# The opening of a delta-rule attention + maxout-FFN kernel: inverse norms, the first transposed solution and the first weights in another order

## The chip, the cores and the metric

The kernel runs on one core of one Trainium2 chip. The metric is device time in microseconds (us), from launch to the last store. The engines are TensorE (PE, matrix products), VectorE (DVE), ScalarE (ACT), GpSimd (POOL) and SyncE (SP, which here only issues transfers). Each works through its own queue of instructions in order; they meet at semaphores. ACT and POOL can issue transfers too.

## What is computed

Two layers follow one another. The first is a delta rule: for each of 4 x 8 heads a 48 x 48 state is carried over 768 tokens. The second is a feed-forward layer (FFN) with the maximum of three products.

```python
k_n = k / (norm(k) + 1e-06)
for t in range(S):
    y[t] = q[t] @ state
    v_old = k_n[t] @ state
    state = state + beta[t] * outer(k_n[t], v[t] - v_old)
x = y.transpose(0, 2, 1, 3).reshape(B * S, H * D)          # 3072 x 384
h = maximum(maximum(x @ w1, x @ w2), x @ w3)               # 384 -> 768
out = h @ w_out                                            # 768 -> 384
```

## The kernel before, in words

**Chunks and groups.** Tokens are taken in chunks of 64. A unit is one chunk of half of the batch; two units make a chunk c of all heads, two chunks make a group m of 512 tokens of the FFN (there are 6 groups). Inside a chunk the recurrence is a triangular system: with A the products of the keys among themselves, u = (I + A)^-1 (scaled values - keys x state). `gram` makes A and the masked products of queries and keys (`pts`) on PE, `turn` transposes keys and queries on PE for that, and ACT or DVE copy each result out of PSUM.

**The solve.** The inverse is found on DVE for blocks of 32 x 32, all heads and blocks at once: each of the 128 partitions holds one block of 1024 numbers. `solve(m)` first takes the key norms from the blocks' diagonals (`norm`), makes the inverse squares times beta (`bl`), scales the blocks with them (L547), puts `bl` on the diagonal of the result (L538), and then runs column by column: a product into `tmp` (L561), a subtraction from the result `y_bl` (L565). For group 0 the blocks are solved only in halves of 16 (`FINE`), so there are 15 steps instead of 31, and the off-diagonal parts are made on PE from the halves: `halves_z` (p_e, L685), `halves_u` (p_f, written back negated at L700). The 32-wide parts of a chunk come from `join_z` (p_z, L713) and `join_u` (p_j, L726, L728). These read the solution in `ut[c]`, and a transposed copy of parts of it: `fine[c]`, made by `halves_t(c)`, and `t1[c]`, made by `turn_t1(c)`, both with the 32 x 32 transposing of DVE.

**From the blocks to ut.** For group 0 the whole 128 x 1024 solution is transposed on DVE (L573), and `placed(cc, i)` copies a quarter of chunk cc into `ut[cc]` (L505, 32 partitions x 512 elements). Chunk 0 is copied at the end of `solve(0)`, by DVE and ACT; chunk 1 in pieces further on. For later groups this goes through DRAM.

**Values.** The system works with unnormalised keys, so the values are scaled by the key norms: `first_norms` transposes the norms of group 0 (L311, DVE), `scale(c)` multiplies v_t by them on POOL (L296). `new(c)` then makes u (p_u, L771) from v_t and ut, `to_y` the chunk's y (p_y, L813), `to_x` transposes y on PE (p_x, L832), ACT copies it to `xt`, and the FFN's products (p_h, L1224) read that. `step` adds to the state (p_s, L794; st, L801).

**Weights.** The weights come as pieces of 128 x 384 in a 64-bit format (`fetch`, on the queues of SP or POOL). The generator `weights()` converts one piece a turn: three ACT operations (L247 to L249) into `mant` and `up`, two buffers each; then `joined` shifts on DVE (L259) and adds on POOL (L263). `joined` of a piece is called in the turn of the next one.

**Order.** All of it is under a schedule written by hand: the program order is the order of each engine's queue. After the first loads, lines 1309 to 1375 write out the opening; then `ffn(0)` is a generator, and after each of its steps i the tables (`FIRST`, `EARLY_LINKS`, `CONVERTED`) say what else is put in: S a step of `solving`, M a masking (DVE), T and P a `turn` and a `gram` of queries, e, f, d, z, j, u, y, x, s, k, q the links of the recurrence. `solve(1)` runs on DVE meanwhile; its y_p lies in PSUM.

PSUM tiles of the opening come from `ps_two`, three buffers of two banks; each p_t, p_g, p_e and so on takes one and holds it until it has been copied out. The square tiles (`square`, 17 buffers) hold the products A (`ats`), the masked ones (`pts`), the `fine` tiles and the FFN's h.

## Time and profile before

Three runs: 506.24 us median (505.86 to 509.44). The profile is one execution.

| | us |
|---|---|
| time of the profiled execution | 506.9 |
| span of its instructions | 505.2 |
| PE busy | 484.0 (96%) |
| DVE busy | 361.1 (71%) |
| POOL busy | 187.1 (37%) |
| ACT busy | 169.4 (34%) |

How to read the lines: an engine's line in the 40 slices has one digit for each slice of 12.6 us, the busy share in tenths; PEclk is the clock that was granted to PE, in tenths of full speed. In the timeline each row is: start, duration, engine, line of the kernel, operation, out<-in by the program's names, shape, how many; in brackets the idle time of the engine before it and what ended it. In the chain of waits each piece has start, duration and the engine, tile and line that held the end up. What an engine names as its releaser is inferred from the last semaphore; where that one had long been done, it was another.

### The profile page before, as it was taken

How to read it: one execution, taken by the hardware profiler on the slowest of the kernel's cores; microseconds unless marked ns; L12 is line 12 of the kernel's file. 1: busy time of each engine (PE TensorE's matmuls, PEld its weight loads, DVE VectorE, ACT ScalarE, POOL GpSimd, SP SyncE). 2: the span in 40 equal slices, each digit the busy share in tenths (PEclk: the TensorE clock that was granted, in tenths of full speed). 3: DMA queues.
4: the chain of work that ended last, by engine and by line, in shares of the span. 5: the costliest groups of instructions: out<-in, count | busy, mean ns of one | idle time of the engine just before them, and what ended most of it. 6: DMA issues, size and time to landing. Idle time of an engine off the chain costs nothing.

```text
span 505.2 us, 18676 instructions
## 1 busy us (share of the span) xinstructions
PE 484.0 (96%) x8064; PEld 338.0 (67%) x8064; DVE 361.1 (71%) x835; ACT 169.4 (34%) x320; POOL 187.1 (37%) x311
## 2 busy tenths in 40 slices
PE   7678989999999999999999999999999999999996
PEld 6467767855566555565565565555797457998895
DVE  5888799787996441799652999565998874468753
ACT  5585664885422142210152200242201032212210
POOL 7434472793391935770395880501000020000000
PEclk9855899999999999999999999999999999999999
DMA  8937869864045934544584652744224230340002
GB/s 114 205 50 214 195 142 160 198 181 137 3 120 134 191 72 77 146 119 117 112 156 104 158 137 74 149 72 96 64 54 90 47 86 15 85 94 1 0 18 47
DMA packets 109121, 53.50 MB, mean 106 GB/s; under 512 B 92208, under 2 KB 102864, under 8 KB 109040
## 3 DMA queue, kind: packets, MB, share of 16 engines
q1 hardware_dynamic: 97280, 31.78, 31.0%
q0 software_dynamic: 9216, 19.85, 16.5%
q8 instruction: 63, 1.03, 0.9%
q10 hardware_dynamic: 2544, 0.69, 0.8%
q14 instruction: 18, 0.15, 0.1%
HBM read 39.17 MB, written 13.11 MB: 103 GB/s over the span
## 4 chain that ended last, share of the span: by engine, by line
PE 76%; DVE 11%; ACT 4%; DMA 3%; SPq 3%; issue 2%; POOL 0%; DVEq 0%; ACTq 0%; POOLq 0%
PE p_h L1224 28%; PE p_o L985 13%; PE p_o L1262 12%; PE p_c L1163 5%; DVE tmp L561 3%; PE p_g L415 2%; PE p_m L905 2%; PE p_u L771 2%; PE p_k L743 2%; DVE y_p L565 2%; DMA kmore<-in_k_dram 2%; PE p_y L813 2%; PE p_s L794 2%; PE p_q L743 1%; PE p_j L726 1%
## 5 line engine op out<-in xcount | busy, mean ns | idle before, releaser
L1224 PE MATMUL p_h<-xt,w_sb 128*128 128x512 f32 (+1 forms) x450 | 186.8, 558 | 0.6 <-ACT xt L839 0.6
L1224 PEld LDWEIGHTS p_h<-xt,w_sb 128*128 128x128 f32 x450 | 82.4, 193 | 69.2 <-issue 61.6
L1238 DVE TENSOR_TENSOR h<-h,p_h 128x512 f32<-128x512 f32 (+1 forms) x42 | 25.5, 607 | 46.8 <-PE p_h L1224 46.3
L565 DVE TENSOR_TENSOR y_bl<-y_bl,tmp 128x31 f32<-128x31 f32 (+20 forms) x139 | 50.4, 363 | 4.8
L561 DVE TENSOR_TENSOR tmp<-x_bl,y_bl 128x31 f32<-128x31 f32 (+20 forms) x139 | 48.8, 351 | 3.9
L1262 PE MATMUL p_o<-wo_sb,h 128*128 128x384 f32 x144 | 48.9, 490 | 0.0
L373 POOL DMA_DIRECT2D turned<-in_q_dram x72 | 39.3, 554 | 4.6 <-POOL turned L368 3.1
L1262 PEld LDWEIGHTS p_o<-wo_sb,h 128*128 128x128 f32 x144 | 26.7, 190 | 17.2
L1234 ACT ACTIVATE h<-p_h 128x512 f32<-128x512 f32 x24 | 14.3, 597 | 69.2 <-PE p_h L1224 69.2
L263 POOL TENSOR_TENSOR w_sb<-mant,up 128x384 int32<-128x384 int32 x18 | 19.0, 1054 | 39.5 <-DVE mant L259 37.8
L415 PEld LDWEIGHTS p_g<-kqt 48*64 48x64 f32 x1216 | 24.5, 142 | 9.2 <-issue 6.3
L415 PE MATMUL p_g<-kqt 48*64 48x64 f32 (+1 forms) x1216 | 27.7, 241 | 0.9 <-ACT kqt L344 0.8
L1268 ACT COPY o_sb<-p_o 128x384 f32<-128x384 f32 x12 | 5.8, 479 | 62.6 <-PE p_o L1262 56.5
L801 DVE TENSOR_TENSOR st<-st,p_s 48x768 f32<-48x768 f32 (+1 forms) x18 | 17.1, 949 | 12.7 <-PE p_s L794 12.4
L399 DVE TENSOR_TENSOR pt<-p_g,mask 128x512 f32<-128x512 f32 x20 | 13.8, 690 | 17.0 <-PE p_g L415 16.9
L598 POOL DMA_DIRECT2D ut<-y_d x4 | 2.6, 653 | 60.6 <-DMA y_d<-y_bl 60.6
L148 POOL DMA_DIRECT2D v_t<-in_v_dram x14 | 11.6, 832 | 35.3 <-PE p_u L771 35.3
L368 POOL MEMSET turned<- 128x96 f32 x18 | 3.3, 191 | 49.4 <-DVE kqt L389 49.4
L771 PEld LDWEIGHTS p_u<-v_t,ut 64*64 64x64 f32 x768 | 13.5, 141 | 8.4 <-issue 7.3
L432 ACT COPY at<-p_g 128x512 f32<-128x512 f32 x22 | 12.8, 585 | 17.4 <-DVE pt L399 15.4
L373 POOL DMA_DIRECT2D turned<-in_k_dram x32 | 17.5, 556 | 1.2 <-POOL turned L368 1.2
L1163 PE MATMUL p_c<-xt,w_sb 128*128 128x256 f32 x72 | 17.7, 379 | 0.0
(239 smaller groups left out, 907.3 us busy)
## 6 DMA issues: line engine op xcount, KB each, us to landing
w_bits<-in_moe_w_dram SPq DMA_DIRECT2D x9, 384.0 KB, 6.2
w_bits<-in_moe_w_dram POOLq DMA_DIRECT2D x9, 384.0 KB, 5.7
turned<-in_q_dram POOLq DMA_DIRECT2D x72, 48.0 KB, 2.8
out_dram<-o_sb SPq DMA_DIRECT2D x36, 96.0 KB, 2.3
y_x<-y SPq DMA_DIRECT2D x32, 96.0 KB, 3.0
qall<-y_x SPq DMA_DIRECT2D x32, 96.0 KB, 2.8
v_t<-in_v_dram POOLq DMA_DIRECT2D x14, 192.0 KB, 5.0
at_d<-at SPq DMA_DIRECT2D x72, 32.0 KB, 3.0
```

What stands on the lines that cost most here:

```text
L263: nc.gpsimd.tensor_tensor(out=dst.bitcast(I32), in0=mant_v.bitcast(I32), in1=up_v, op=ALU.add)
L373: (queue, nc.gpsimd)[i].dma_start(out=t[p0 : p0 + 32, bb, at : at + NP * 2 * D].rearrange("p (j x) -> p j x", j=NP), in_=(k, q)[i][2 * bb ...
L415: nc.tensor.matmul(p_g[rows(bb ^ (g * i)), par, c0 : c0 + C * (1 + whole)], kq[:, 0], kq if whole else kq[:, i],)
L561: nc.vector.tensor_tensor(out=t_v, in0=row.to_broadcast(t_v.shape), in1=column.to_broadcast(t_v.shape), op=ALU.mult,)
L565: nc.vector.tensor_tensor(out=rest, in0=rest, in1=t_v, op=ALU.subtract)
L771: nc.tensor.matmul(p_v[rows(bb ^ g), g, i], ut[c % NU][rows(bb), g, h], rhs[rows(bb), g, h],)
L801: nc.vector.tensor_tensor(out=s_v[r], in0=s_v[r], in1=p_s[r, :, 0 : H * D], op=ALU.add)
L985: nc.tensor.matmul(to[:, g], a[j][:, 128 * g : 128 * (g + 1)], b[j], start=(start and g == j == 0), stop=(stop and g == 1 and j == len(a) ...
L1163: nc.tensor.matmul(to, w[stays], moves, start=(n == 0), stop=(n == len(terms) - 1))
L1224: nc.tensor.matmul(p_h, w_sb[i][:, t, f * 128 : (f + 1) * 128], xt[:, t, lo : lo + w], start=(t == 0), stop=(t == KT - 1),)
L1238: nc.vector.tensor_tensor(out=h, in0=h, in1=p_h, op=ALU.max)
L1262: nc.tensor.matmul(p_o, stays, moves, start=(n == 0), stop=(n == len(terms) - 1))
```

## The change

- `inverse_squares` takes the place of `norm`, a second reciprocal and a squaring for group 0: with s = |k|^2 and e = 1e-6, (sqrt(s) + e)^2 = s + 2 e sqrt(s) + e^2 is made with one ACT root and one DVE operation; a reciprocal follows. The norms themselves, which only the values need, are made by `first_roots`: a root on ACT, and on POOL one refining step in four operations of 128 x 32.
- The whole transposing of group 0's solution (L573) becomes `turn_back(1)`, `turn_back(0)` of a half each. The half that p_e reads (`high`) is placed in ut[0] first, by DVE and ACT. `fine` is no longer a transpose of ut: `turn_half` transposes the first half of the solution once more in the other direction, and `halves_t(c, engines)` copies eight small parts (32 x 8 x 16) into tiles that POOL has set to zero (`zero_halves`). The low half is turned and placed after `halves_z(0)`.
- The first two weight pieces are converted on ACT earlier, between the copies of the opening's grams; the joins are called apart (`join_first`), the first of them after `turn_t1(0)` and `first_norms`.
- `placed(1, ...)`, which stood in pieces among the work of chunk 0 (one on POOL), stands behind `to_y(0)`, all on DVE.
- `turn(3, (1,))` moves behind `to_x(0)`, and `gram(3, (1,))` into the FFN's step 3, where it writes its masked product straight from PSUM (P3) instead of a copy and a masking (M3).
- Both copies of z in `halves_z` are on ACT.
- `to_x(0)` stands ahead of the start of `solve(1)`.

```diff
-        waiting = None
...
-            if waiting:
-                joined(*waiting)
-            waiting = dst, mant, mant_v, up_v
+            waiting.append((dst, mant, mant_v, up_v))
             yield
-        joined(*waiting)
-        yield
+    waiting = deque()
+    def join_first():
+        joined(*waiting.popleft())
...
+    def inverse_squares(out, square_of, ksum):
+        nc.scalar.activation(
+            out=square_of, in_=ksum, func=mybir.ActivationFunctionType.Sqrt,
+            scale=4.0 * EPS * EPS,
+        )
+        nc.vector.scalar_tensor_tensor(
+            out=square_of, in0=square_of, scalar=EPS * EPS, in1=ksum,
+            op0=ALU.add, op1=ALU.add,
+        )
+        nc.vector.reciprocal(out, square_of)
+    def first_roots():
+        out, square_of, inverse = bl_0
+        t, mult = small("root_bl", BL), nc.gpsimd.tensor_tensor
+        nc.scalar.sqrt(out, square_of)
+        mult(out=t, in0=out, in1=out, op=ALU.mult)
+        mult(out=t, in0=t, in1=inverse, op=ALU.mult)
+        nc.gpsimd.tensor_scalar(
+            out=t, in0=t, scalar1=-0.5, scalar2=1.5, op0=ALU.mult, op1=ALU.add
+        )
+        mult(out=out, in0=out, in1=t, op=ALU.mult)
...
+    ys = []
+    def turn_back(s):
+        cols = slice(HB * s, HB * (s + 1))
+        nc.vector.transpose(
+            out=in_rows(xs[0])[:, cols], in_=ys[0].rearrange("p c i -> p i c")[:, cols]
+        )
-    def placed(cc, i, copy=nc.vector.tensor_copy, xs_of=slice(0, 2 * H)):
+    def placed(cc, i, copy=nc.vector.tensor_copy, cols=slice(0, BL)):
...
         if m == 0:
-            back = in_rows(xs[0])
-            nc.vector.transpose(out=back, in_=y.rearrange("p c i -> p i c"))
-            yield
-            for i in range(4):
...
+            ys.append(y)
             return
...
-    def halves_t(c, parts=(0, 1)):
...
+    def zero_halves(c):
+        fine[c] = [square("t") for g in range(2)]
+        zeros(*fine[c])
+    def first_half():
+        return in_wo(1)[:, 0, 0 : HB * BL].rearrange("p (c x) -> p c x", x=BL)
+    def turn_half():
+        nc.vector.transpose(
+            out=first_half().rearrange("p c x -> p (c x)"),
+            in_=ys[0][:, 0:HB].rearrange("p c i -> p (c i)"),
+        )
+    def halves_t(c, engines):
+        for n, engine in enumerate(engines):
+            f, bb, g = n // 4, n // 2 % 2, n % 2
+            x0 = 16 * c + 8 * g
+            copy = nc.scalar.copy if engine is nc.scalar else engine.tensor_copy
+            copy(
+                fine[c][g][block(bb ^ g, f), :, BL * f : BL * f + HB],
+                first_half()[block(bb, f), :, x0 : x0 + H].rearrange("p c h -> p h c"),
+            )
...
     load_beta()
+    first_roots()
+    zero_halves(0)
+    zero_halves(1)
     keys(6)
     gram(0, (1,), None, later=True)
     turn(7, (0,))
+    some(conv, 1)
     turn(1, (1,))
     keys(7)
     turn(2, (1,))
     gram(1, (1,), None, later=True)
-    turn(3, (1,))
     some(conv, 1)
     gram(2, (1,), None, later=True)
-    gram(3, (1,), None, later=True)
-    some(solving, HB + 1)
-    halves_t(0)
+    some(solving, HB)
+    low, high = slice(0, HB), slice(HB, BL)
+    turn_back(1)
+    for i in range(4):
+        placed(0, i, A.copy if i % 2 else V.tensor_copy, high)
+    turn_half()
+    halves_t(0, (V, A, V, A, V, A, V, V))
     halves_z(0)
+    turn_back(0)
+    for i in (1, 3, 0, 2):
+        placed(0, i, V.tensor_copy, low)
+    halves_u(0)
+    turn_t1(0)
     first_norms()
-    some(conv, 1)
-    placed(1, 0)
+    join_first()
     scale(0, nrm_0[:, 0])
-    placed(1, 1, nc.gpsimd.tensor_copy)
     blocks(1, nc.gpsimd)
     for _ in range(2):
         fetch(nc.gpsimd)
-    halves_u(0)
-    turn_t1(0)
     join_z(0)
     masked(pts[0], by_par(pts[0]))
-    placed(1, 2)
     join_u(0)
     masked(pts[1], by_par(pts[1]))
     old_k(0)
     old_q(0)
     new(0)
     some(conv, 1)
+    join_first()
     fetch(nc.gpsimd)
     load_v(1, nc.gpsimd)
-    placed(1, 3)
     to_y(0)
-    halves_t(1)
+    for i in (0, 2, 3, 1):
+        placed(1, i)
+    halves_t(1, (V, V, V, V, V, V, V, V))
     solving = solve(1)
+    to_x(0)
+    join_first()
+    some(conv, 1)
     some(solving, 1)
-    to_x(0)
-    some(conv, 1)
+    turn(3, (1,))
...
-        3: "j1 S1 q1 M3 S1 S1", 4: "u1 T4", 5: "y1", 6: "s1 T5", 7: "x1 T6",
+        3: "j1 S1 q1 P3 S1 S1", 4: "u1 T4", 5: "y1", 6: "s1 T5", 7: "x1 T6",
```

In the FFN's loop `join_first()` stands behind each `some(conv, 1)`.

More of the change, by code (lines that the diff above doesn't have):

```diff
@@ L277, in norm @@
         )
+    EPS = 1e-6
+    def inverse_squares(out, square_of, ksum):
[18 more added lines that the diff above has]
+        mult(out=out, in0=out, in1=t, op=ALU.mult)
     def small(name, *shape):
@@ L504, in placed @@
         of = in_rows(xs[0])[r, :, 16 * cc : 16 * (cc + 1)].rearrange("p i x -> p x i")
-        copy(to[:, xs_of], of[:, xs_of])
+        copy(to[:, :, cols], of[:, :, cols])
     def solve(m):
@@ L521, in solve @@
         bl = small("bl", BL)
-        norm(bl, diagonal(x), small("root_bl", BL), small("nt_bl", BL))
-        if m == 1:
-            y = ps_two("y_p").rearrange("p b (j i) -> p (b j) i", i=BL)
-            nc.scalar.copy(y, zero.to_broadcast(y.shape))
         if m:
+            norm(bl, diagonal(x), small("root_bl", BL), small("nt_bl", BL))
+            if m == 1:
+                y = ps_two("y_p").rearrange("p b (j i) -> p (b j) i", i=BL)
+                nc.scalar.copy(y, zero.to_broadcast(y.shape))
             norms_of(m, bl)
             nc.vector.reciprocal(bl, bl)
+            nc.vector.tensor_tensor(out=bl, in0=bl, in1=bl, op=ALU.mult)
         else:
-            bl_0.append(bl)
-            bl = small("inv_bl", BL)
-            nc.vector.reciprocal(bl, bl_0[0])
-        nc.vector.tensor_tensor(out=bl, in0=bl, in1=bl, op=ALU.mult)
-        nc.vector.tensor_tensor(out=bl, in0=bl, in1=beta_bl[:, m] if m else beta_0, op=ALU.mult)
+            bl_0.extend((bl, small("square_bl", BL), small("inv_bl", BL)))
+            bl = small("nt_bl", BL)
+            inverse_squares(bl_0[2], bl_0[1], diagonal(x))
+        nc.vector.tensor_tensor(
+            out=bl, in0=bl if m else bl_0[2], in1=beta_bl[:, m] if m else beta_0,
+            op=ALU.mult,
+        )
         if m > 2:
@@ L571, in solve @@
         if m == 0:
-            back = in_rows(xs[0])
-            nc.vector.transpose(out=back, in_=y.rearrange("p c i -> p i c"))
-            yield
-            for i in range(4):
-                if i % 2:
-                    n = H * (i == 3)
-                    if n:
-                        placed(0, i, nc.vector.tensor_copy, slice(0, n))
-                    placed(0, i, nc.scalar.copy, slice(n, 2 * H))
-                else:
-                    placed(0, i, nc.vector.tensor_copy)
+            ys.append(y)
             return
@@ L637 @@
     fine = {}
-    def halves_t(c, parts=(0, 1)):
-        if c not in fine:
-            fine[c] = [square("t") for g in range(2)]
-        src = [ut[c % NU][:, g].rearrange("p h x -> p (h x)") for g in range(2)]
-        dst = [t.rearrange("p h x -> p (h x)") for t in fine[c]]
-        if 0 in parts:
-            nc.vector.transpose(out=dst[0], in_=src[0])
-        for bb in range(2) if 1 in parts else ():
-            nc.vector.transpose(out=dst[1][rows(1 - bb)], in_=src[1][rows(bb)])
+    def zero_halves(c):
[16 more added lines that the diff above has]
+                first_half()[block(bb, f), :, x0 : x0 + H].rearrange("p c h -> p h c"),
+            )
     def heads_of(c, name, w):
@@ L676, in halves_z @@
     def halves_z(c):
-        if c > 1:
-            halves_t(c)
         at = [ats[2 * c + g] for g in range(2)]
@@ L687, in halves_z @@
                     )
-            copy(zs[c % NU][:, :, span(hs)], p_v)
+            nc.scalar.copy(zs[c % NU][:, :, span(hs)], p_v)
     def halves_u(c):
@@ L1464 @@
         if i == 25:
-            some(conv, 1)
+            join_first()
         if i == 21:
@@ L1474 @@
             some(conv, 1)
+            join_first()
         if i == 0:
```

## The prediction

> **What bounds the kernel now.** I read the 40 slices first: TensorE (PE) is full nearly everywhere except the first tenth, and its granted clock dips there. Then the windows, the chain of waits through that tenth, and last the timeline of VectorE (DVE), ScalarE (ACT) and GpSimd (POOL) there.

> ```profile
> PE   7678989999999999999999999999999999999996
> PEclk9855899999999999999999999999999999999999
> ```
> ```profile
> 25.00:30.00 5.00, 2.58 (x68) 2.22 (x68) 4.71 (x10) 3.94 (x7) 0.00 (x0) 0.58 0.58 103
> 35.00:40.00 5.00, 4.68 (x195) 4.15 (x195) 4.66 (x8) 3.69 (x11) 4.62 (x6) 0.50 0.20 69
> 50.00:53.10 3.10, 3.10 (x60) 2.74 (x53) 1.49 (x5) 1.92 (x4) 2.96 (x3) 0.50 0.85 151
> 53.10:60.00 6.90, 6.56 (x209) 5.09 (x208) 4.78 (x14) 4.22 (x9) 2.73 (x3) 1.00 0.71 194
> ```
> After each stretch: length, then busy us of PE, weight loads, DVE, ACT, POOL, then the clock. PE runs at 0.50 up to 53.1, at 1.00 after.

> ```profile
> 26.43 2.00 DVE x_bl L573
> 28.45 0.60 DVE ut L505
> 29.05 1.03 ACT ut L505
> 30.10 0.64 ACT ut L505
> 30.78 1.07 PE p_e L685 x29
> ...
> 38.10 1.14 PE p_u L771 x32
> ...
> 44.92 2.93 PE p_h L1224 x6
> ```
> In this chain (start, length, what) the solution is transposed whole, copied into place, used by p_e, and eventually by p_u; the FFN starts at 44.92. After 53 us PE is busy 26.96 of 30.00 (60 to 90), 20.00 of 20.00 (90 to 110) and 390 of 395, so what the opening wins or loses should reach the end. The question is therefore what happens to 44.92, and to the second solve, whose DVE loop begins at 52.4.

> ```profile
> 16.93 0.69 DVE L547 TENSOR_TENSOR x_bl<-x_bl,inv_bl 128x512 f32<-128x512 f32 x1
> 36.55 1.53 DVE L399 TENSOR_TENSOR pt<-pt,mask 128x512 f32<-128x512 f32 x1
> 39.17 0.69 DVE L399 TENSOR_TENSOR pt<-pt,mask 128x512 f32<-128x512 f32 x1
> ...
> 17.03 0.69 POOL L538 COPY y_bl<-inv_bl 128x32 f32<-128x32 f32 x1 [2.63 <-DVE inv_bl L534]
> 33.79 1.21 POOL L263 TENSOR_TENSOR w_sb<-mant,up 128x384 int32<-128x384 int32 x1 [12.56 <-DVE mant L259]
> 34.97 1.47 POOL L296 TENSOR_TENSOR v_t<-v_t,nrm 128x768 f32<-128x768 f32 x1
> 36.50 1.03 POOL L505 COPY ut<-x_bl 32x512 f32<-32x512 f32 x1
> ```
> Two lessons. The values v_t are scaled by 36.44, 1.66 us before p_u needs them. And DVE and POOL block one another: L538, a copy of 32 columns, lasts 0.69 because L547 runs until 17.62; L399 takes 1.53 instead of 0.69 because L505 on POOL runs until 37.53.

> **One-root inverse squares.** From the root at 14.33 to L534's end at 16.89 now. After: root 0.26, one two-input DVE operation (0.19 to 0.22 in L273, L274), reciprocal 0.35, product 0.19, gaps of 0.03: done by 15.43. Solve starts **1.46 earlier**. L534's four 50 ns semaphore waits then pass during the reciprocal; if not, +0.2.

> **Roots and zeros on POOL.** They stand behind y_bl, load_q(3) and load_beta (issue ends at 21.2 now, 19.8 then), so inside the solve (16.3 to 24.9), whose operations read two SBUF tiles each. No row shows a 32-column arithmetic operation of POOL: L538 took 0.11 after its release, L263 about 2.6 ns a column, so 0.11 to 0.2. Four such cost DVE between 0 (they slip into gaps) and 0.8; I take 0.5, as L399 was blocked for all of L505's remainder. The four memsets of 512 columns are about 0.5 each (0.42 for 384, 0.97 for 1056 columns); 0 to 2.0 on DVE, and I take 0: the 0.97 memset ran beside the 1.98 transpose L480, which took no longer than L573 alone. That transpose has one input, so the upper end stays in the range. [...] Solve ends at 26.40 - 1.46 + 0.5 = 25.45.

> **Halves, and conversions moved.** First half transposed: 1.0 (half of L573), to 26.45. ACT now has both conversions before it. The second w_bits, issued 0.67 after the first, landed at 22.4; the first's landing is not recorded: I take 21 (bounds 18.9, 22.4). Conversion 21.0 to 22.6, three copies and a pt of 0.59 to 24.95, conversion to 26.5, pt to 27.1. Then two ut copies of 256 elements at 0.64: 28.4, against 30.73 now. p_e's halves, 1.1 each at half clock: 29.5, 30.6. Meanwhile DVE does its copies (0.37 each), the transpose of y (0.71) and five small t copies (0.26 from 0.59 at 512 and 0.37 at 256), done by 29.4; ACT three at 0.43, to 29.7, then z. p_f's first half 30.6 to 31.7, so L700's work starts at 31.7, not 33.70: **-2.0**. The low half's transpose and copies (1.0 + 4 x 0.37) hide on DVE before p_f's second half at 32.7. turn_t1 (36.52 now) ends at about 34.8: -1.7, and ut would let p_u start at 36.35.

> **The new wait.** first_norms and the first weight join now stand behind turn_t1 on DVE, and scale behind the join on POOL. So: 34.8 + 0.21 (L311) + 0.03 + 0.35 (L259) = 35.4; hand-over 0.15; L263 takes 0.99 to 1.31, but the masked product issued on DVE at 35.4 holds it off to 36.05: done 36.9 (without that 36.4); scale 1.47: **v_t at 38.4**, with bounds 37.7 and 39. p_u starts there, 0.3 later than now. Behind scale on POOL wait blocks(1), two fetches and load_v, 0.9 later; their readers (root_bl at 46.8, the fourth conversion at 45.2, the next scale at 52) still cover that.

> **From p_u to the second solve.** p_y, y and p_x follow 0.3 later. turn(3,(1,)) now stands between p_x and p_h: four transposes, 1.0 at half clock, where PE idles 0.57 for xt: +0.5. p_h starts at 45.7, **+0.8**; p_e, p_s, then st at +0.8 on PE's side. On DVE, y ends at 43.0; then four placements on ut (2.4; three stood earlier in idle time, one on POOL), eight t copies (2.3, was 2.1), and join, norms and scaling (4.8 as now) give 52.5 for st instead of 51.51, +1.0; its idle 1.89 before st is used up. DVE waits for p_k at 55.9 anyway, so PE's +0.8 counts. gram(3,(1,)), 32 matmuls (0.55), moves into the FFN: mostly into PE's gaps of 1 us at 65.6 and 85.8, while one masked product reads PSUM and so escapes a block (1.12 at 63.37 against 0.69). I charge +0.1.

> z's second copy on ACT, load_q(6) behind turn(3) on SP, and ACT's root and zero copy behind xt cost nothing: ACT is idle there (1.91 busy of 5 in 45 to 50), and load_q(6) issues 2 us after that turn; uncovered they'd cost 0.4, 1 and 1.3.

> Sum: +0.8 + 0.1 = +0.9 on the profiled execution (span 505.2, 506.9 with what lies around it): 507.8. The median of the runs, 506.24, is 0.66 below that execution, so **507.1**.

> **Rivals.**
> *Faster: the values are ready in time.* If scale finishes before ut does, because turn_t1 or the join runs earlier than I put it, p_u starts at 36.35, -1.75; turn(3) gives back 0.5, so -1.25 on PE's side, and DVE's 9.5 us from y (40.9) to st leaves st at 50.4, -1.1, the later of the two. With the 0.1: -1.0, **505.2**. It decides if v_t comes before 37.3. For: 36.44 now. Against: the order on DVE and POOL, which is fixed.
> *Slower: the memsets block the solve.* Place: POOL beside L561/L565 in the first solve. Price up to 2.0, and turn_t1 and v_t move with it: **509.1**. It decides if those tmp/y_bl rows grow beside memsets. For: L399's block. Against: L480's row.
> *The clock returns at another time.* Now at 53.1, after p_s and p_h. One p_h group costs 2.40 at half and 1.56 at full clock, a 64-matmul block 1.93 and 1.15: one of each earlier or later is 1.6, so **505.5 or 508.7**.
> *The change does nothing visible*: all its effects cancel at p_h, 506.2; this lies inside the range.

> **Numbers.** My forecast (506.3 to 508.2) 0.45; values in time 0.25; memsets or a later landing of the first weights 0.15; clock 0.15. Range 504.4 to 509.6: from the faster case less 0.8 (clock half-way) to the slow one plus 0.5. Every case lies inside 1% (501.2 to 511.3), about what this kernel's runs (505.86 to 509.44) can tell from no change. Beyond it are two cases added together: faster 0.05, slower 0.05.

> **What would show it.** Right: L547's successor at 15.5; the solve's last row near 25.4; p_e at 28.4; v_t's scaling ending between 37.7 and 39 and p_u just after it; p_h at 45.7; the clock back at 1.00 within 3 us of 53. Wrong: scale ending before the last p_j, a p_u that waits for ut, first-solve rows over 0.4, or ACT idle at the first conversion past 22.4.

## The result, and the profile after

The changed kernel is slower: 509.7 us median of 22 runs against 507.2 of 22 runs of the kernel before on the same chip, a ratio of 1.005 (95% interval 1.0029 to 1.0071). That is +2.5 us where +0.9 was forecast, and 0.1 beyond the upper end of the range. The profiled execution took 512.0 (span 510.3; before 506.9 and 505.2). Single executions of one kernel lie up to 7 us apart (504.7 to 511.7 before, 507.4 to 512.8 of the changed kernel, one slow one of 515.9 left aside), so the traces are read for places and the runs for the size.

The 40 slices of the changed kernel, to be laid beside those of before:

```profile
PE   7759799999999999999999999999999999999996
PEclk9756689999999999999999999999999999999999
```

A slice is 12.8 us. PE's third digit is 5 (before 7), its fifth 7 (before 9): two new holes, at 26 to 38 and at 51 to 64. The clock is a little better in the fourth slice (6, before 5) and worse in the fifth and sixth (6 and 8, before 8 and 9).

The same windows as before (length, busy us of PE, weight loads, DVE, ACT, POOL, clock, DMA):

```profile
25.00:30.00 5.00, 2.50 (x82) 2.18 (x76) 4.64 (x11) 4.88 (x11) 0.00 (x0) 0.50 0.69 129
35.00:40.00 5.00, 2.39 (x103) 2.25 (x98) 1.36 (x3) 1.76 (x5) 4.24 (x4) 0.50 0.11 17
50.00:53.10 3.10, 1.89 (x41) 1.36 (x39) 2.85 (x9) 0.86 (x2) 1.47 (x1) 1.00 1.36 180
53.10:60.00 6.90, 5.79 (x121) 4.56 (x124) 5.92 (x17) 3.04 (x7) 1.74 (x2) 0.60 1.06 196
```

From 35 to 40 PE, DVE and ACT stand still for much of the time while POOL works: PE is busy for 2.39 of 5 where it was 4.68. From 50 to 53.1 the clock is at 1.00, earlier than before (0.50), and PE uses it for 1.89 of 3.10; it was full there. After 53.1, where the clock was at 1.00 before, it is at 0.60. So the changed kernel gets its clock back sooner, idles, and loses it again.

The chain of waits through the opening (start, length, engine, tile, line):

```profile
27.74 0.62 ACT ut L540
...
28.41 1.92 PE p_e L725 x60
30.33 1.78 PE p_f L736 x62
...
33.73 0.43 DVE t L660
...
34.79 1.30 POOL w_sb L263
36.09 1.90 POOL v_t L322
...
38.04 1.15 PE p_u L811 x32
...
51.84 2.20 DVE wo_sb L585
54.04 0.88 DVE st L841
...
54.96 1.96 PE p_k L783 x64
```

p_e has all of ut at 28.41 where before it was 30.78, so the opening gains 2.4 us; then join and scaling on POOL set p_u, at 38.04 where it was 38.10. p_h (the FFN's first products) starts at 44.92 in both kernels. The loss stands behind it. The timeline of all engines there (start, duration, engine, line, operation, tiles; in brackets the idle time ahead and what ended it):

```profile
48.12 0.99 POOL L263 TENSOR_TENSOR w_sb<-mant,up 128x384 int32<-128x384 int32 x1 [3.14 <-ACT kqt L370]
48.48 0.72 DVE L273 TENSOR_TENSOR nt_bl<-nt_bl,wo_sb 128x32 f32<-128x32 f32 x1
...
51.12 0.77 PE L736 MATMUL p_f<-z,t 64*64 64x32 f32 x35
...
51.49 1.47 POOL L322 TENSOR_TENSOR v_t<-v_t,nrm 128x768 f32<-128x768 f32 x1 [1.67 <-DMA v_t<-in_v_dram]
...
51.75 2.29 DVE L585 TENSOR_TENSOR wo_sb<-wo_sb,bl 128x1024 f32<-128x1024 f32 x1
...
53.96 0.94 DVE L841 TENSOR_TENSOR st<-st,p_s 128x768 f32<-128x768 f32 x1
...
54.03 0.75 PE L736 MATMUL p_f<-z,t 64*64 64x32 f32 x29 [2.14 <-issue]
...
54.96 1.96 PE L783 MATMUL p_k<-st,kqt 48*64 48x48 f32 x64 [0.18 <-DVE st L841]
```

The same steps in the timeline of DVE and PE in the kernel before (its L547 is L585 of the changed kernel, L801 is L841, L696 is L736):

```profile
45.53 0.21 DVE L273 TENSOR_TENSOR nt_bl<-nt_bl,wo_sb 128x32 f32<-128x32 f32 x1
48.14 1.22 DVE L547 TENSOR_TENSOR wo_sb<-wo_sb,bl 128x1024 f32<-128x1024 f32 x1
...
51.51 0.95 DVE L801 TENSOR_TENSOR st<-st,p_s 128x768 f32<-128x768 f32 x1 [1.89 <-PE p_s L794]
...
53.70 1.14 PE L696 MATMUL p_f<-z,t 64*64 64x32 f32 x64
...
65.65 0.49 PE L771 MATMUL p_u<-v_t,ut 64*64 64x48 f32 x17 [1.01 <-issue]
```

Two things are late. DVE's step on the state (L841, st) starts at 53.96 instead of 51.51: L273 and L585 take 0.72 and 2.29 beside POOL's L263 and L322, and took 0.21 and 1.22 before, when POOL was idle (its scaling of that chunk ran beside L801 then, which kept its 0.95). And PE stops for 2.14 us in the middle of p_f's 64 matmuls, with no releaser ("issue"); before, they ran without a stop. The two end together: the rest of p_f is done at 54.78 and st at 54.90, and p_k stands behind the one on PE and reads the other, so that taking away one of them alone wins little by p_k. Two lines of the profile's page say what the stop can be:

```profile
PE 487.2 (95%) x8064; PEld 340.1 (67%) x8064; DVE 361.8 (71%) x842; ACT 168.9 (33%) x324; POOL 188.5 (37%) x318
...
q8 instruction: 63, 1.03, 0.9%
```

PE has 2 x 8064 = 16128 matmuls and weight loads, and queue q8 carries 63 packets, 1.03 MB, 16.4 KB each: 256 such instructions a packet. (With the waits and branches of PE's sequencer the trace has 16262, so the match of 16128 with 63 x 256 is not exact evidence; the distances between the gaps are.) Counted through the trace with the sequencer's, the three such gaps of PE before 70 us (2.14 at 54.0, 0.95 at 61.3, 0.90 at 66.9) fall on its instructions 1987, 2242 and 2499, 256 apart to within one. I read them as the ends of blocks of 256 instructions at which PE waits for the next block; no row names a packet as what ends a gap. The packet that fits the first gap, the seventh of q8, ran from 50.44 to 52.11, and PE went on 1.9 us after it; the eighth and ninth end at 59.82 and 65.42, 1.5 us ahead of the ends of the other two gaps. The kernel before has one such gap ahead of 70 us, 1.01 at 65.65.

That block came later in the changed kernel, and not only PE earlier. The seventh packet ran from 47.78 to 49.30 in the kernel before and from 47.87 to 49.45 in its second execution (e11 below); in the changed kernel it was 50.44 to 52.11, and 49.56 to 51.01 in the second (e10). With a packet that ends at 49.30, and the same 1.9 us behind it, PE could by estimate have gone on from 51.2, which is ahead of its arrival there at 51.89. What made the fetch start later is not shown.

### The profile page after: what moved, and what is told of

It reads as the page before. It is cut to its first block, busy times and chain, and to the rows that moved or that the text cites. A ratio compares the mean times of both kernels' runs of the same rounds, so it can differ in the third digit from the quotient of the medians.

```text
span 510.3 us, 18693 instructions
## 1 busy us (share of the span) xinstructions
PE 487.2 (95%) x8064; PEld 340.1 (67%) x8064; DVE 361.8 (71%) x842; ACT 168.9 (33%) x324; POOL 188.5 (37%) x318
## 3 DMA queue, kind: packets, MB, share of 16 engines
q8 instruction: 63, 1.03, 0.9%
HBM read 39.17 MB, written 13.11 MB: 102 GB/s over the span
## 4 chain that ended last, share of the span: by engine, by line
PE 82%; DVE 5%; DMA 4%; ACT 3%; POOL 2%; SPq 2%; issue 2%; DVEq 0%; POOLq 0%
PE p_h L1264 31%; PE p_o L1025 12%; PE p_o L1302 12%; PE p_c L1203 5%; PE p_g L441 3%; PE p_u L811 2%; PE p_k L783 2%; PE p_m L945 2%; PE p_y L853 2%; PE p_q L783 2%; SPq L129 2%; PE p_s L834 2%; DMA v_t<-in_v_dram 1%; PE p_j L766 1%; PE p_z L753 1%
## 5 line engine op out<-in xcount | busy, mean ns | idle before, releaser
L1264 PE MATMUL p_h<-xt,w_sb 128*128 128x512 f32 (+1 forms) x450 | 189.9, 566 | 0.0
L1264 PEld LDWEIGHTS p_h<-xt,w_sb 128*128 128x128 f32 x450 | 84.1, 197 | 68.9 <-issue 61.6
L1278 DVE TENSOR_TENSOR h<-h,p_h 128x512 f32<-128x512 f32 (+1 forms) x42 | 25.5, 606 | 46.8 <-PE p_h L1264 46.4
L399 POOL DMA_DIRECT2D turned<-in_q_dram x72 | 39.1, 551 | 5.3 <-POOL turned L394 2.9
L1302 PEld LDWEIGHTS p_o<-wo_sb,h 128*128 128x128 f32 x144 | 26.7, 190 | 17.2
L263 POOL TENSOR_TENSOR w_sb<-mant,up 128x384 int32<-128x384 int32 x18 | 18.5, 1030 | 40.9 <-DVE mant L259 24.4
L841 DVE TENSOR_TENSOR st<-st,p_s 48x768 f32<-48x768 f32 (+1 forms) x18 | 17.1, 949 | 10.8 <-PE p_s L834 10.5
L148 POOL DMA_DIRECT2D v_t<-in_v_dram x14 | 11.5, 829 | 35.7 <-PE p_u L811 35.7
L399 POOL DMA_DIRECT2D turned<-in_k_dram x32 | 17.5, 553 | 1.2 <-POOL turned L394 1.2
L811 PE MATMUL p_u<-v_t,ut 64*64 64x48 f32 x768 | 14.8, 228 | 3.2 <-POOL v_t L322 2.6
```

The costliest lines, as they stand in the source:

```text
L263: nc.gpsimd.tensor_tensor(out=dst.bitcast(I32), in0=mant_v.bitcast(I32), in1=up_v, op=ALU.add)
L399: (queue, nc.gpsimd)[i].dma_start(out=t[p0 : p0 + 32, bb, at : at + NP * 2 * D].rearrange("p (j x) -> p j x", j=NP), in_=(k, q)[i][2 * bb ...
L811: nc.tensor.matmul(p_v[rows(bb ^ g), g, i], ut[c % NU][rows(bb), g, h], rhs[rows(bb), g, h],)
L1264: nc.tensor.matmul(p_h, w_sb[i][:, t, f * 128 : (f + 1) * 128], xt[:, t, lo : lo + w], start=(t == 0), stop=(t == KT - 1),)
L1278: nc.vector.tensor_tensor(out=h, in0=h, in1=p_h, op=ALU.max)
L1302: nc.tensor.matmul(p_o, stays, moves, start=(n == 0), stop=(n == len(terms) - 1))
```

## An account of the time behind p_h

For 19 of the traces (all that are told of below but e17_all_later's) I took D, the time from the first p_h to the first p_z of the second group, PE's idle time in it, and the time at half clock. A least-squares fit gives D = 53.6 + 0.95 x idle + 0.38 x half clock, and what it leaves has a standard deviation of 0.4 us. The 0.38 is a little below what the rows give: a p_h group of 2.93 at half clock (56.85 in the changed kernel) takes 1.56 at full (49.63), so a microsecond at half clock loses 0.47; a block of 64 matmuls, 1.93 and 1.15, loses 0.40. The group of 2.40 that the prediction priced as half clock, at 51.37 in before, runs over the change of the clock at 53.1.

| execution (us) | p_h | D | PE idle | of it "issue" | half clock | p_z of the second group |
|---|---|---|---|---|---|---|
| before | 44.92 | 60.0 | 3.3 | 1.0 | 8.2 | 104.9 |
| before, again (e11) | 44.48 | 59.5 | 2.4 | 1.0 | 8.7 | 103.9 |
| changed | 44.92 | 64.1 | 4.2 | 4.0 | 16.3 | 109.1 |
| changed, again (e10) | 44.56 | 62.1 | 4.2 | 3.1 | 9.9 | 106.7 |
| e1_scale_first | 42.55 | 66.1 | 7.2 | 3.9 | 13.6 | 108.6 |
| e3_both | 43.08 | 60.9 | 4.2 | 3.9 | 8.0 | 104.0 |
| e5_loads_late | 44.53 | 60.5 | 3.8 | 2.5 | 8.4 | 105.1 |
| e6_both_loads_late | 43.55 | 59.3 | 2.4 | 1.5 | 8.8 | 102.9 |
| e7_one_root | 42.61 | 57.0 | 3.6 | 3.6 | 0.0 | 99.6 |
| e18_both_all_later | 43.36 | 62.0 | 3.4 | 0.0 | 14.7 | 105.4 |

On the mean of two executions each, the changed kernel has 1.35 us more PE idle time behind p_h and 4.7 us more at half clock: 0.95 x 1.35 + 0.38 x 4.7 = 3.1 of the 3.4 by which D grew. At p_h the two kernels are level (44.7). Two more executions with the opening of before, e9_before_loads_late's and e15_before_f1_later's, have p_h at 47.59 and 47.93, but there the whole opening starts late: the block of 64 p_g matmuls that starts at 12.54 and 12.14 in before and e11 starts at 15.34 and 14.99. Counted from that block, p_h follows after 32.3 to 32.9 us in the four executions with the opening of before and after 32.1 to 32.2 in four with that of the changed kernel (the changed one, e10, e5, e13). So the change gains 0.4 there by the means, 0.2 without e15.

## The experiments

**The values' wait, DVE's queue, the moved gram.** Theory V: the scaling of the values, which holds p_u until 38.0, costs the opening its lead. Theory D: the four placements of the second chunk make DVE late for st. Theory T: turn(3) and gram(3) in their new places cost.

e1_scale_first:

```diff
     halves_z(0)
...
+    first_norms()
+    scale(0, nrm_0[:, 0])
...
-    first_norms()
     join_first()
-    scale(0, nrm_0[:, 0])
```

> The values are scaled ahead of the first weight join (first_norms and scale behind the copies for p_e), all else as in the changed kernel, which measured 1.005 of the kernel before. Theory V (the cost is the values' wait, 38.04 instead of some 36.1 for p_u): p_u starts at 36.0 to 36.3, p_h near 43.1, the time falls by 1.5 to 2, ratio 1.001 to 1.002. Theory D (the cost is DVE's queue ahead of the second solve, 11.5 us from y to st): st comes earlier only as far as y does, it stays the last thing before p_k, and DVE's gap before p_k remains; ratio 1.002 to 1.004. Theory T (the moved turn and gram): no change, 1.005.

```profile
29.51 1.47 POOL L322 TENSOR_TENSOR v_t<-v_t,nrm 128x768 f32<-128x768 f32 x1 [6.17 <-DVE nrm L337]
...
36.03 2.27 PE L811 MATMUL p_u<-v_t,ut 64*64 64x48 f32 x62 [0.47 <-issue]
```

In the timeline of e1_scale_first the scaling is done at 30.98, p_u starts 2.0 earlier and p_h at 42.55, 2.4 earlier. The runs: 1.0009 (0.9981 to 1.0037), 509.1 us, against 1.005. V holds: the wait is worth about 0.4% (the two intervals, taken together, leave 0.1 to 0.8). The profiled execution itself is a poor one (3.88 us of "issue" at 65.4), which is why the table has it at 108.6.

e2_placed_early, and e3_both, which is e1_scale_first with the placements 0 and 2 after masked(pts[1]), 3 ahead of to_y(0) and 1 behind it:

```diff
     masked(pts[1], by_par(pts[1]))
+    for i in (0, 2, 3, 1):
+        placed(1, i)
...
     to_y(0)
-    for i in (0, 2, 3, 1):
-        placed(1, i)
```

> The four copies of chunk 1 into ut stand behind the second masked product, where DVE idles from 36.7 to 40.1 in the changed kernel, instead of between y and the second solve. Theory D: st comes 2.4 to 3.4 earlier than 53.96 (also because the scaling of x no longer meets POOL's scaling of v_t), PE no longer stands before p_k, the time falls by 2 to 3, ratio 0.999 to 1.001. Theory V: p_u stays at 38.0 and p_h at 44.9, so the time does not move, 1.004 to 1.006. Theory C (the fall of the clock at 54.5 is the cost): if PE no longer stands at 52 to 54, the clock stays at 1.00 after its first return and the fall is larger, ratio below 0.998.

> Both edits: values scaled first, and chunk 1's copies in DVE's idle time (two behind the second masked product, one behind u, one behind y). V and D each alone would leave the other's cost; if both are real and add up, p_u at 36.1, p_h at 43.1, st near 50, and a ratio of 0.993 to 0.997, faster than both kernels. If V or D is empty, the ratio is that of the other edit alone.

e2_placed_early: 1.0046 (1.0029 to 1.0063), though st comes at 52.44, 1.5 earlier. PE then stops 1.95 at p_f just the same. D alone wins nothing: the stop at p_f ends no sooner. e3_both: 0.9988 (0.9963 to 1.0013), 507.4 us, the best of the versions of the changed kernel; p_h at 43.1, 1.8 earlier than before, st at 49.4. A lead of 1.8 would be 0.9965; most of it is gone by the end. The gap at p_f is there, 2.08 at 51.4, and half clock from 51.1 to 58.0.

e4_turn3_back takes turn(3, (1,)) and gram(3, (1,)) back into the opening (with M3 in place of P3 in the FFN's step 3):

```diff
     turn(2, (1,))
     gram(1, (1,), None, later=True)
+    turn(3, (1,))
     some(conv, 1)
     gram(2, (1,), None, later=True)
+    gram(3, (1,), None, later=True)
...
-    turn(3, (1,))
```

> turn(3) and gram(3) of the queries stand in the opening again (with the copy on ACT and the masking later), all else as in the changed kernel. Theory T (0.5 for the turn before p_h, 0.55 for the gram in the FFN): the time falls by about 1, ratio 1.003. Against it: the turn waits for a load that landed at 24.7, PE and ACT do it before the first p_e, so p_e starts later, by 0.5 to 1.5: ratio 1.005 to 1.008. V and D: no change, 1.005.

1.0043 (1.002 to 1.0067). T falls: their new places cost nothing that the runs can tell. With them back, p_e's bulk starts at 30.15 instead of 28.41, as the trace of one execution has it.

**The transfers.** From 50 to 53.1 the DMA share is 1.36 where it was 0.85. Theory F: the fetch of PE's block stands in line with the loads of q, k and weights, and the stall it brings costs twice, as idle time and as clock.

e5_loads_late; e6_both_loads_late is the same on e3_both, e9_before_loads_late on the kernel before:

```diff
-        if i == 1:
+        if i == 3:
             load_q(4)
             load_q(5)
-        if i == 2:
+        if i == 4:
             load_q(6)
```

> The changed kernel with the loads of q and k for the next group (load_q(4), load_q(5)) issued at i = 3 of the FFN's loop in place of 1, and load_q(6) at 4 in place of 2: fewer data transfers between 47 and 53 us. In the changed kernel PE stood still for 2.14 us before p_f at 54.0 with nothing to wait for, at the point where its 1987th instruction is reached, while a fetch of an instruction block on queue q8 took 1.67 us in place of 1.25; the clock went to half again for 10 us. Theory F (the block's fetch is held up by the data transfers): the stall falls below 1 us, the second stretch of half clock shrinks, 1 to 3 us less than the changed kernel: ratio to the kernel before 0.999 to 1.003. Rival P (the stall is set by the pace of PE against the 256 instructions of a block, the loads have nothing to do with it): stall 2 us as before, ratio 1.005.

> e3_both with the same two loads issued later. e3_both gave 0.9988 with p_h at 43.1 (1.8 earlier than before), a stall of 2.08 at p_f and a second stretch of half clock of 6.8 us. Theory F: stall under 1 us, ratio 0.993 to 0.997. Rival P: 0.999, stall 2 us.

> The kernel before with load_q(4) and load_q(5) at i = 3 and load_q(6) at i = 4: the control for e5_loads_late, where the same move took the changed kernel from 1.005 to 1.000. If the move relieves a stall that the change itself brought in (theory F: the changed kernel reaches its 1987th PE instruction and that block's fetch in the stretch where these loads run), the kernel before gains nothing, 0.999 to 1.002. If the loads cost any kernel the same (rival L), it gains 2 to 3 us too, 0.994 to 0.997, and e5_loads_late says nothing about the change.

The timeline of PE in e5_loads_late:

```profile
51.79 0.66 PE L736 MATMUL p_f<-z,t 64*64 64x32 f32 x29 [0.81 <-issue]
53.69 1.96 PE L783 MATMUL p_k<-st,kqt 48*64 48x48 f32 x64 [1.24 <-DVE st L841]
```

e5_loads_late: 1.000 (0.9979 to 1.002), 507.9 us; the block's packet took 1.07 in place of 1.67 and 1.45, and the gap at p_f is 0.81 in place of 2.14 and 1.18. e9_before_loads_late: 0.9999 (0.9983 to 1.0014). So the same move is worth 0.5% to the changed kernel and nothing to the kernel before: it takes away a cost that the change brought in. That this cost is the block's fetch is not shown. The expectation set the packet's 1.67 against 1.25, which is the time of the next block's packet; the same block's took 1.52 and 1.58 in the two executions of before, so against that the changed kernel's 1.67 and 1.45 are not slow. And the later loads help by a second way: POOL's scaling of v_t, which waits for its own load, starts at 49.61 in e5_loads_late in place of 51.49 and 50.38. It then holds DVE's L564 for 0.52 in all, instead of L585 for 2.29 or L564 for 1.28, and st is done at 53.64 in place of 54.90 and 54.42. PE waits for st after the stop at p_f in all three traces, so up to p_k it is st that sets the time, and a shorter stop alone would have won nothing there. In part the expectation missed, too: a second stretch of half clock, 6.8 us, is still there. And e6_both_loads_late is 0.9994 (0.9973 to 1.0014), no better than e3_both, though its stop at p_f is 0.29 where e3_both's was 2.08: what the values' wait and the later loads are worth does not add.

**The same two kernels again.**

> The changed kernel once more, for a second profiled execution. If the values' wait is a matter of the program, v_t ends at 38 and PE's gap there is 2.5 us again; if the stall at p_f and the second stretch of half clock are too (theory F), PE stops again for 1.5 to 2.5 us near 54 and the clock is at half again for 6 to 10 us after it. If these two belong to the one execution (rival), neither need come, and its ratio of 1.005 must be sought elsewhere.

> The kernel before once more, for a second profiled execution: p_h at 44.9 and no gap of PE over 1 us without a releaser before 60 if its opening is a matter of the program; half clock from 26 to 53 if that is, too; a start of the second group's first p_z within 1 us of 104.9.

e10_after_again: 1.0049 (1.0022 to 1.0076). Its timeline:

```profile
50.38 1.47 POOL L322 TENSOR_TENSOR v_t<-v_t,nrm 128x768 f32<-128x768 f32 x1 [1.06 <-DMA v_t<-in_v_dram]
...
50.62 1.28 DVE L564 TENSOR_TENSOR bl<-bl 128x32 f32<-128x32 f32 x1
...
52.87 0.66 PE L736 MATMUL p_f<-z,t 64*64 64x32 f32 x29 [1.18 <-issue]
54.47 1.96 PE L783 MATMUL p_k<-st,kqt 48*64 48x48 f32 x64 [0.94 <-DVE st L841]
```

The stop at p_f, the wait for st and the second half-clock stretch (54.5 to 61.3) belong to the program. Only which row on DVE is blocked differs: here the product of 32 columns, 0.19 by itself, lasts until POOL's scaling is done at 51.85. e11_before_again has p_h at 44.48, half clock until 53.2, and no gap without releaser of over 0.5 us before 65.

**One root alone.** e7_one_root is the kernel before with `inverse_squares` and `first_roots` and nothing else of the change; e12_root_loads_late adds the later loads.

> The kernel before with the one-root inverse squares alone. The first solve starts and ends 1.3 to 1.5 us earlier (end near 25.0, before 26.40). If the opening's lead passes through to the end: p_h at 43.5, ratio 0.997 to 0.998. If it is lost after p_h (an instruction block's fetch, a later clock): p_h at 43.5 too, ratio 0.999 to 1.002, with a PE gap of over 1 us without a releaser before 60 us.

> e7_one_root with the loads moved as in e5_loads_late, the version that the runs point to: e7_one_root had p_h 2.3 us earlier than the kernel before and yet 0.9996, with PE gaps without a releaser of 0.7, 1.4 and 1.5 at 48.6, 52.9 and 62.3. Theory F (blocks' fetches behind the loads eat the lead): gaps before 60 under 1 us, ratio 0.994 to 0.997. Rival (the lead is lost by the clock, or later): 0.999 to 1.001.

e7_one_root 0.9996 (0.9962 to 1.0029), e12_root_loads_late 1.0006 (0.9975 to 1.0037): no gain, though the first solve ends at 25.0 and 25.1 in place of 26.4. e16_root_f1_later (its edit is further down) shows in its timeline where the lead is lost:

```profile
25.65 0.63 PE L364 MATMUL p_t<-ident,qall 128*128 128x128 f32 x4 [2.92 <-DMA qall<-in_q_dram]
...
26.31 0.59 ACT L370 COPY kqt<-p_t 128x512 f32<-128x512 f32 x1 [2.93 <-PE p_t L364]
...
29.29 1.70 ACT L531 COPY ut<-x_bl 32x512 f32<-32x512 f32 x2
...
30.39 0.43 PE L714 MATMUL p_e<-ut,at 64*64 64x32 f32 x6 [2.30 <-ACT ut L531]
```

ACT's placement of ut stands behind the copies of turn(3), and that turn waits for load_q(3) to land: p_e at 30.39. In e12_root_loads_late the same turn starts at 25.15, behind the gram's copies on ACT, and p_e at 30.35; the two executions of before have 30.13 and 29.55. Only in e7_one_root's did the turn run at 22.9, and p_e started at 28.07 (span 501.0). In the changed kernel, where turn(3) has moved, p_e starts at 27.8 and 26.7 in its two executions, and at 29.5 in e4_turn3_back, which puts it back.

**Filling PE's idle time.** Theory C: PE's idle time at 51 to 60 brings the second half-clock stretch. The windows in the steps of that clock, 3.41 us, first of before, then of the changed kernel, then of e18_both_all_later (busy us of PE first, the clock third from the end):

```profile
46.27:49.68 3.41, 3.41 (x76) 2.58 (x78) 3.10 (x10) 0.41 (x2) 0.00 (x0) 0.50 0.89 197
49.68:53.09 3.41, 3.41 (x72) 3.05 (x65) 1.48 (x5) 2.14 (x4) 3.19 (x3) 0.50 0.84 149
53.09:56.51 3.42, 3.42 (x135) 2.93 (x135) 1.50 (x4) 1.54 (x5) 1.74 (x2) 1.00 0.85 234
```

```profile
47.62:51.04 3.42, 3.42 (x135) 3.01 (x134) 3.17 (x11) 2.77 (x6) 1.70 (x2) 1.00 1.08 155
51.04:54.45 3.41, 1.27 (x63) 1.08 (x64) 3.24 (x6) 0.00 (x0) 1.47 (x1) 1.00 1.29 169
54.45:57.86 3.41, 3.23 (x82) 2.83 (x74) 2.60 (x8) 2.18 (x6) 1.71 (x2) 0.50 1.13 204
```

```profile
51.24:54.65 3.41, 2.10 (x81) 1.82 (x74) 3.14 (x13) 2.25 (x6) 1.74 (x2) 1.00 1.19 186
54.65:58.06 3.41, 2.53 (x68) 1.61 (x66) 3.27 (x10) 1.91 (x5) 0.32 (x1) 0.50 0.65 168
```

A window with PE busy for 1.27 (1.30 in e10_after_again, 1.63 in e3_both, 2.10 here) is followed by one at half clock. Before, PE is busy for all of 46.27 to 53.09 at half clock, and after 53.1 the clock stays at 1.00.

In the clock records of the traces of before and of the changed kernel each stretch is at 0.50 or at 1.00, and all but the last are 3.41, 6.83, 10.24, 13.65, 27.31, 436.91 and 450.56 us long, which are 1, 2, 3, 4, 8, 128 and 132 times 3.413. How much idling takes the clock away is not shown by them: half clock follows the windows with 1.27 to 2.10 us of work, and one with 2.51 (64.69 to 68.10 in the changed kernel), while 1.00 follows one with 2.40 (63.33 to 66.74 in before).

e8_warm is e3_both with dummy matmuls ahead of the opening's p_e, whose results nobody reads:

```diff
+    busy(3, ident)
     turn(7, (0,))
...
+    busy(4, ident)
     halves_z(0)
```

> e3_both with dummy matmuls on PE (busy(3) ahead of turn(7,(0,)), busy(4) ahead of halves_z(0)), whose results nobody reads, to fill PE where it idles at 20 to 29 us. Theory C (the clock goes to half because PE idles at 20 to 29, and comes back sooner if it does not): the half-rate stretch that ended at 44.3 in e3_both ends earlier or does not begin, 1 to 3 us less, ratio 0.993 to 0.997. Rival (the small matmuls of 30 to 40 us keep the clock at half whatever stands ahead): 0.999 or a little more, half clock to 44.

1.0031 (1.0002 to 1.006): worse than e3_both. Half clock lasts until 43.8, as in the rival; the gap at p_f is 3.07. It falls behind 20 of p_f's matmuls, in e3_both behind 34: the 14 dummy matmuls ahead move the end of the block forward by as many, which agrees with blocks of a fixed count.

e13_f1_later puts a due group of p_h between p_s and p_f; e14_both_f1_later does so on e3_both, e15_before_f1_later on the kernel before, e16_root_f1_later on e7_one_root:

```diff
-        0: "e1 s0 S1 S1", 1: "f1 k1 S1 S1 S1", 2: "z1 d1 M2 S1 S1",
+        0: "e1 s0 S1 S1", 1: "S1 S1 S1", 2: "f1 k1 z1 d1 M2 S1 S1",
```

> The changed kernel with p_f and p_k of the second chunk (f1 k1) issued one step of the FFN later, so that a group of p_h (1.5 us at full clock) stands between p_s and p_f where PE idled 2.14 and 1.18 us in its two profiles. Theory C (PE's idle time there brings the second stretch of half clock, and that costs 0.4 us a us): the gap at p_f falls below 0.7, the second stretch of half clock is 3.4 us or none, ratio 0.998 to 1.001. Rival D (DVE's second solve is late by itself, PE's idle time is only its sign): half clock or not, p_z of the second group starts at 106.7 or later, ratio 1.004 to 1.006.

> e3_both with the same move; e3_both had 0.9988, a gap of 2.08 at p_f and 6.8 us of half clock from 51.1. C: no second stretch or 3.4 us of it, ratio 0.994 to 0.997. D: 0.998 to 1.001.

> The kernel before with the same move: the control. PE has no idle time between 45 and 55 there, so by C nothing is won: 0.999 to 1.002 (more if DVE, which waits 1.6 us for p_k there, waits longer). If it wins 1 us or more too (below 0.998), the order of p_f and p_h matters to any opening, and e13 says nothing of the change.

> e7_one_root with the same move. e7_one_root was 0.9996 with gaps without a releaser of 0.7, 1.4 and 1.5 (48.6, 52.9, 62.3) and no second stretch of half clock in its profile. C: in other executions it has one, which the move prevents, 0.995 to 0.998. D: 0.999 to 1.001.

1.0073 (1.0047 to 1.01), 1.0016 (0.9994 to 1.0039), 1.001 (0.9981 to 1.0039) and 0.9985 (0.9958 to 1.0012). The first two are a little slower than both C and D had forecast. e13_f1_later's timeline says why it is no fair test of C:

```profile
52.45 0.77 PE L736 MATMUL p_f<-z,t 64*64 64x32 f32 x36 [0.40 <-issue]
...
56.42 0.54 ACT L246 ACTIVATE mant<-w_bits 128x384 f32<-128x384 f32 x1 [6.32 <-POOL w_sb L263]
...
57.83 1.51 ACT L740 ACTIVATE ut<-p_f 16x256 f32<-16x256 f32 x4
...
59.40 0.81 PE L753 MATMUL p_z<-ut,at 32*32 32x32 f32 x44 [4.04 <-ACT ut L740]
```

The gap at p_f is nearly filled (0.40; none in e14_both_f1_later), but p_f's result now stands on ACT behind a conversion that waits 6.3 us for POOL, and PE is idle for 4.04 at p_z instead. Half clock follows again.

e17_all_later (on the changed kernel) and e18_both_all_later (on e3_both) put all of the second chunk's steps one FFN step later, and that conversion off:

```diff
-        0: "e1 s0 S1 S1", 1: "f1 k1 S1 S1 S1", 2: "z1 d1 M2 S1 S1",
-        3: "j1 S1 q1 P3 S1 S1", 4: "u1 T4", 5: "y1", 6: "s1 T5", 7: "x1 T6",
-        8: "T7", 14: "P4", 15: "P5", 21: "P6", 22: "P7",
+        0: "e1 s0 S1 S1", 1: "S1 S1 S1", 2: "f1 k1 S1 S1", 3: "z1 d1 M2 S1 S1 S1",
+        4: "j1 q1 P3", 5: "u1 T4", 6: "y1", 7: "s1 T5", 8: "x1 T6",
+        9: "T7", 14: "P4", 15: "P5", 21: "P6", 22: "P7",
...
-        if i in CONVERTED:
+        for _ in range({1: 0, 5: 2}.get(i, int(i in CONVERTED))):
             some(conv, 1)
             join_first()
```

> The changed kernel with all steps of the first group's second chunk from p_f on one step of the FFN later (f1 k1 at 2, z1 d1 at 3, and so on to T7 at 9), and the weight conversion of step 1 moved to step 5, so that p_f's result on ACT does not stand behind it. Theory C (PE's idle time at 51 to 60 brings the second stretch of half clock, which costs 0.4 us a us): gaps of p_f and p_z below 1 us, second stretch 3.4 us or none, ratio 0.998 to 1.002. Rival D (DVE's second solve is late by itself): 1.004 to 1.006 whatever the clock does.

> e3_both with the same two moves. C: no stretch of half clock after 50, ratio 0.994 to 0.997, the version to keep. D: 0.998 to 1.001.

e17_all_later 1.0029 (1.0003 to 1.0054), between what C and D had forecast, and without a profile that shows its usual course; e18_both_all_later 0.9997 (0.9966 to 1.0028), the range of D, with 13.7 us of half clock from 54.7, where C had none. The timeline of PE in the latter:

```profile
51.69 1.15 PE L783 MATMUL p_k<-st,kqt 48*64 48x48 f32 x64 [0.22 <-DVE st L841]
53.92 2.25 PE L1264 MATMUL p_h<-xt,w_sb 128*128 128x256 f32 x6 [1.09 <-POOL w_sb L263]
...
58.77 2.93 PE L1264 MATMUL p_h<-xt,w_sb 128*128 128x256 f32 x6 [1.59 <-POOL w_sb L263]
```

No "issue" is left, and PE waits for the weights' joins on POOL instead, 1.1 and 1.6. Each time one idle stretch was filled another came: a gap without releaser, ACT, POOL, st. What they share is DVE, busy 4.75, 4.72, 4.69 and 4.73 of 5 us from 50 to 55 in the changed kernel, e10, e13 and e18, against 2.38 before: once PE has its full clock at 44 to 48, DVE is nearly full there and PE is not. That DVE's work is the bound is not shown by this, since e2_placed_early, with st 1.5 earlier, won nothing; and no run kept PE from idling at 51 to 60, so C rests on the account and on some of the windows, not on a run that removes its cause. Also open is why e6_both_loads_late, whose trace has the second group's p_z 1.0 to 2.0 earlier than before, comes out level in the runs; two executions of the changed kernel differ by 2.4 us at that point, so one trace can't settle it.

## Why the prediction was too low

**Right.** The first solve's first row at 16.45 (16.3 forecast) and its end at 25.10 (25.45). The conversions from 21.34 (21.0), ACT's placements done at 28.36 (28.4). The work after p_f at 31.25 (31.7) and turn_t1's end at 34.2 (34.8). The new wait, the main risk named: v_t at 37.99 (38.4, bounds 37.7 and 39), p_u just after it. e1_scale_first shows that this wait is what holds p_u, and that without it the changed kernel is about 0.4% faster. That is the faster rival's mechanism; yet with it gone the time is that of before (1.0009) and not 1.0 less, so that rival's sum was too good as well.

**Too dear, without harm.** The roots on POOL were charged 0.5; the first solve's rows stay at 0.29 and less beside them, so they cost nothing here, and the four memsets, 1.92 us from 21.45, cost nothing either (the rows beside them last 0.26 to 0.29, and those of the same widths ahead of them as long): the slower rival falls. The roots did not hold DVE in the changed kernel's two profiles, and by 0.08 at most in others (one row of 0.29 took 0.37 in e16_root_f1_later and 0.34 in e5_loads_late). turn(3) between p_x and p_h was charged 0.5; p_x starts 0.3 earlier than before, since ACT's zeroing no longer stands ahead of y, and p_h starts at 44.92 and 44.56, not 45.7.

**The step that failed** is the one from p_h to the second solve: "DVE waits for p_k at 55.9 anyway, so PE's +0.8 counts", with +0.1 for all that comes behind. The +0.8 did not come: at p_h the change costs nothing. The +0.1 did not hold: behind p_h it costs 3.4 us in the profiles. Three things were missing or too small:
- st was put at 52.5 and came at 53.96 and 53.47. The term that was mis-sized is the 4.8 for join, norms and scaling on DVE: from the join's shift to st it took 6.36 (47.60 to 53.96) and 6.37 in e10, 1.5 of it by blocks of POOL's join and of its scaling of the second chunk (0.5 and 1.1). Such blocks were priced in the opening and not looked for here, where DVE, busy 4.75 of 5 us from 50 to 55, now works on while POOL does. So p_k waits for DVE, and not DVE for p_k. By itself this lateness was worth nothing in the runs (e2_placed_early), since PE's stop at p_f remained.
- "The clock returns at another time" was taken as one step earlier or later, 1.6 of either sign. It did return earlier (47.6), so PE came to p_f sooner than it could go on there, the packet itself ending 1.6 to 2.8 later than before, and to p_k before st was made. PE idled, and the clock went down a second time, for 10.2 and 6.8 us; that the idling is what took the clock away is my reading of the windows and was not shown by a run.
- What I read as the wait for an instruction block was in the trace of before, as one gap of 1.01 with no releaser at 65.65, and was put at nothing. In the changed kernel such gaps make 4.0 and 3.1 us.

The sizes by the runs: without the values' wait 0.4% less, with the loads out of the way 0.5% less, and the two do not add. How the 2.5 us divide among st, the instruction blocks and the clock stays open.

Of the 2.6 us between the forecast of 507.1 and the 509.7 measured, 1.0 is the kernel before itself: the forecast started from 506.24, the median of three runs, and the 22 runs have 507.2. The other 1.6 is the change, +2.5 where +0.9 was forecast. So 509.7 lies outside the likeliest case, 506.3 to 508.2, and just outside the whole range, and it is the shifted start that put it outside. The chances in the forecast add up to 1.10, as the two cases of 0.05 were counted on top of the rest.

## What to carry to other kernels

Here an edit that let PE arrive sooner, and have its full clock sooner, was worth what the others could supply there. Before crediting such an edit, look in the stretch that it runs into, and not only in the one that it shortens, for DVE's share (4.75 of 5 us from 50 to 55 here), for DVE's rows beside POOL's joins and scalings (L585 at 2.29 where it was 1.22) and for PE's gaps marked "issue" (2.14 at p_f). Count the instructions between such gaps (255 and 257 here), and see which transfers run beside the packets. In before PE was full at half clock from 46.27 to 53.09, and st, at 51.51, held nothing up; in the changed kernel the clock was at 1.00 from 47.62, and st, at 53.96, was waited for. Two late things that end together hide each other: removing one of them tells nothing of what both are worth.
